# Linear attention, 32 heads: the last head's exp and relu of q cut into three parts, and new instruction orders on four engines

## The chip, the cores and the metric

The kernel runs on one core of a Trainium2 chip. The metric is the device time of one call in microseconds (us), lower is better. A run is called slow when it lies over 1.5% above the fastest run of the same kernel. "Ratio" is the mean time of one kernel's fast runs over that of the kernel before in the same rounds on the same chip, with a 95% interval; it is not quite the ratio of the medians that are quoted beside it. A profile is one execution; its span is 1.7 to 1.9 us shorter than the device time of the same execution.

## The reference, cut to what matters

```python
q, k, v: bf16, shape (1, 32, 2048, 128)          # 32 heads, 2048 rows, 128 columns
phi_q = where(q > 0, q + 1, exp(q)) + 1e-6       # the kernel: (min(exp(q), 1) + 1e-6) + max(q, 0)
phi_k = where(k > 0, k + 1, exp(k)) + 1e-6
kv  = einsum("bhsd,bhse->bhde", phi_k, v)        # one 128 x 128 matrix a head
z   = einsum("bhsd->bhd", phi_k)
num = einsum("bhqd,bhde->bhqe", phi_q, kv)
den = einsum("bhqd,bhd->bhq", phi_q, z) + 1e-6
return num / den
```

A head is 16 tiles of 128 rows. q, k, v and the output are 512 KB a head each, 67.1 MB in all.

## The kernel before

Every operation has a name such as `T12.0` (head 12, part 0). Each engine executes its own fixed list; semaphores carry the dependences between them. The names:

- SP (the queue of DMA): `ldq`, `ldk`, `ldv` load a head (seven buffers of each), `st` stores one (twelve buffers).
- TensorE (PE): `T` transposes q into PSUM, `kv` sums kv and z, `n` multiplies phi_q by them.
- ScalarE (ACT): `ek`, `eq` exp of k and q, `rqa` relu of the first half of q, `kvs` copies kv out of PSUM.
- VectorE (DVE): `em`, `emq` the min/add behind exp, `rkd`, `rqb` relu of half of k and of q, `r` reciprocal of the denominator, `f` the final multiply.
- GpSimd (POOL): `v1` copies v, `rkp` relu of the other half of k.

```python
NI, NO = 7, 12                                   # input and output buffers, in heads

def q_parts(h):
    return HALVES if h in (0, NH - 1) else WHOLE # HALVES = ((0, 8), (8, 16))

def gate(name, h):                               # GpSimd may start only when VectorE is here:
    if h < 3: return []
    return [f"r{h - 3}.0"] if name == "v1" else [f"f{h - 3}.0"]

# ... VectorE's list, heads 1 to 3 (the fill) and the end:
#   em1.0 r0.0 f0.0 rqb1 rkd2.0 emq1.0 rkd3.0 em2.0 r1.0 em3.0 rqb2 emq2.0 r0.1 f0.1
#   f1.0 rkd4.0 em4.0 rkd5.0 r1.1 rqb3 f1.1 ...
#   ... emq30.0 rqb31 r29.1 emq31.0 f29.1 r30.0 f30.0 r30.1 emq31.1 f30.1 r31.0 ... f31.2
# ... GpSimd's:  v12.0 v13.0 rkp3.0 v14.0 rkp4.0 ...
# ... SP's:      ... ldv12.0 ldq11.0 st1.0 st2.0 ldk13.0 ldv13.0 ldq12.0 ldk14.0 ...
#                ... ldv31.0 st18.0 st19.0 ldq31.0 st20.0 st21.0 ... st31.2

def load(name, dst, src, h, i, t0, t1, last):    # 'last': the buffer has been read
    add("SP", f"ld{name}{h}.{i}", lambda e: e.dma_start(dst[:, h % NI, t0:t1], ...), last, ...)

add("PE", f"T{h}.{i}", g, over("ldq", ...) + ["ident"]
    + ((every("eq", h - 1, q_parts) + rqs(h - 1)) if h else []))   # q loaded, PSUM read out
add("DVE", f"rqb{h}", ... rq_sb[:, h % NQ, n:], xT[:, n:], 0.0, None, op0=ALU.max ...)
```

## Time and profile before

The measurement gave 171.82 us (three runs, 171.63 to 172.05). The profiled run took 172.31 us, so it is one of the longer ones.

| stage of the profiled run | from, to (us) | what sets it |
|---|---|---|
| fill | 0 to 28.8 | loads of the first heads, then VectorE |
| steady | 28.8 to 156.4 | TensorE, 27 heads at 4.726 us |
| drain | 156.4 to 170.4 | VectorE's chain, then the last store |

These are lines of the page of the kernel before: the busy share of the DMA engines in tenths, in 40 slices of 4.26 us, and under it what they moved.

```profile
DMA  5999999999999999999999999999999999999874
GB/s 202 366 417 417 408 406 407 411 404 419 410 407 415 412 407 415 406 402 416 414 416 411 414 420 411 415 419 411 422 413 415 411 415 420 412 411 421 357 304 170
```

DMA is full from the third slice to the 37th, at about 412 GB/s, and falls in the last three.

The table of busy time by stage, of the same kernel, has a start and end in each row, then the length and the busy time of PE, PE's weight loads, DVE, ACT and POOL.

```profile
core 0: us, PE busy (x) PEld busy (x) DVE busy (x) ACT busy (x) POOL busy (x), PEclk, DMA share, GB/s
60.00:100.00 40.00, 40.00 (x732) 39.93 (x730) 39.51 (x70) 40.00 (x36) 22.63 (x17) 1.00 1.03 412
156.00:171.00 15.00, 8.09 (x145) 7.57 (x141) 11.07 (x21) 3.33 (x5) 0.20 (x1) 0.94 0.72 282
```

TensorE never pauses between 60 and 100 us.

The timeline has a start, a duration, then the engine and the instruction; in brackets stands the idle time ahead of it and what ended it. Line L352 holds the transposes, so its first instruction of a head is that head's start on TensorE. Shown are heads 2, 3, 4, 12 and 31, then the first numerator of head 31 and the last multiply.

```profile
16.81 1.07 PE L352 MATMUL la<-la 128*128 128x128 bf16 x16 [0.88 <-DVE la L364]
...
21.55 1.05 PE L352 MATMUL la<-la 128*128 128x128 bf16 x16
...
28.81 1.07 PE L352 MATMUL la<-la 128*128 128x128 bf16 x16 [1.22 <-DVE la L364]
...
66.62 1.05 PE L352 MATMUL la<-la 128*128 128x128 bf16 x16
...
156.40 0.61 PE L352 MATMUL la<-la 128*128 128x128 bf16 x8
...
163.38 0.18 PE L371 MATMUL la<-la 128*128 128x3 bf16 x1 [1.41 <-DVE la L392]
...
166.73 0.69 DVE L392 TENSOR_TENSOR la<-la 128x512 bf16<-128x512 f32 x1
```

Head 4 starts 7.26 us after head 3, against 4.73 in the steady state. The reason is on VectorE and GpSimd, in the same timeline (first the three VectorE instructions, then GpSimd's four of that time):

```profile
21.18 1.57 DVE L357 TENSOR_SCALAR la<-la 128x2048 bf16<-128x2048 bf16 x1
...
25.14 1.17 DVE L326 TENSOR_SCALAR la<-la 128x1024 bf16<-128x1024 bf16 x1
26.23 1.52 DVE L323 TENSOR_SCALAR la<-la 128x2048 bf16<-128x2048 bf16 x1
...
21.16 1.04 POOL L334 COPY la<-la 128x1024 int32<-128x1024 int32 x1 [2.58 <-DVE la L323]
22.17 1.47 POOL L330 TENSOR_SCALAR la<-la 128x1024 bf16<-128x1024 bf16 x1
24.99 1.04 POOL L334 COPY la<-la 128x1024 int32<-128x1024 int32 x1 [1.35 <-issue]
26.00 1.21 POOL L330 TENSOR_SCALAR la<-la 128x1024 bf16<-128x1024 bf16 x1
```

These are emq2, rkd4 and em4 (GpSimd's four are the copy of v3, rkp3, the copy of v4 and rkp4). Where nothing meets them, they take 0.62 to 0.69, 0.36 to 0.43 and 0.68 us; here each began while GpSimd was at work and ended after it. The Trainium skill ("SBUF — State Buffer", Who interferes with whom) says that VectorE in its two-port modes and GpSimd take a shared pair of ports as an exclusive lock for a whole instruction. The trace agrees: emq2 started at 21.18, GpSimd's copy ended at 22.20, and emq2 ended at 22.75, about its own 0.6 us later.

### The profile page before, as it was taken

Reading aid. Unit: us, or ns where it says so; the run is one execution under the profiler, and the core shown is the slowest. Engines: PE = TensorE matmul, PEld = TensorE weight load, DVE = VectorE, ACT = ScalarE, POOL = GpSimd, SP = SyncE. Lnnn points to the kernel's source line nnn. Section 1 sums busy time; section 2 is a strip of 40 time slices with the busy share of each in tenths; the row PEclk is TensorE's granted clock in tenths of the full one; section 3 lists DMA queues with packets and bytes.
Section 4 is the critical chain, followed back from the end, with each engine's and each line's share of the span. In section 5 each row is a group of like instructions: output and inputs, shape, how many; then the busy total and the mean of one; then the engine's idle time right before and its main releaser. Section 6 shows DMA issues by size and latency. Waiting matters only on the chain.

```text
span 170.4 us, 6325 instructions
## 1 busy us (share of the span) xinstructions
PE 159.1 (93%) x2775; PEld 153.7 (90%) x2775; DVE 155.3 (91%) x267; ACT 152.9 (90%) x132; POOL 86.1 (51%) x71
## 2 busy tenths in 40 slices
PE   6997977999999999999999999999999999999950
PEld 2677976999999999999999999999999999999940
DVE  0178999999999999999999999999999999999992
ACT  3699988899999999999999999999999999996700
POOL 1346364565456655556644566456665466654000
PEclk9999999999999999999999999999999999999998
DMA  5999999999999999999999999999999999999874
GB/s 202 366 417 417 408 406 407 411 404 419 410 407 415 412 407 415 406 402 416 414 416 411 414 420 411 415 419 411 422 413 415 411 415 420 412 411 421 357 304 170
DMA packets 18748, 67.53 MB, mean 396 GB/s; under 512 B 2080, under 2 KB 2464, under 8 KB 18720
## 3 DMA queue, kind: packets, MB, share of 16 engines
q1 hardware_dynamic: 18720, 67.12, 98.0%
q8 instruction: 22, 0.36, 0.8%
q14 instruction: 6, 0.05, 0.1%
HBM read 50.33 MB, written 16.78 MB: 394 GB/s over the span
## 4 chain that ended last, share of the span: by engine, by line
PE 83%; DVE 9%; ACT 4%; issue 1%; POOL 0%; POOLq 0%
PE la L341 30%; PE la L376 18%; PE la L352 16%; PE la L378 16%; DVE la L392 4%; ACT la L320 2%; PE la L299 2%; DVE la L323 1%; DVE la L364 1%; ACT la L355 1%; DVE la L357 1%; DVE la L326 1%; DVE la L385 1%; ACT la L361 1%; PE la L371 1%
## 5 line engine op out<-in xcount | busy, mean ns | idle before, releaser
L392 DVE TENSOR_TENSOR la<-la 128x1536 bf16<-128x1536 f32 (+2 forms) x65 | 77.7, 1196 | 0.4
L378 PE MATMUL la<-la 128*128 128x129 bf16 x512 | 68.1, 220 | 0.0
L376 PE MATMUL la<-la 128*128 128x129 bf16 x512 | 68.0, 219 | 0.0
L341 PE MATMUL la<-la 128*128 128x129 bf16 x1024 | 64.2, 219 | 0.0
L355 ACT ACTIVATE la<-la 128x2048 bf16<-128x2048 bf16 (+1 forms) x34 | 60.3, 1778 | 3.5 <-PE la L378 1.8
L334 POOL COPY la<-la 128x1024 int32<-128x1024 int32 (+1 forms) x33 | 40.9, 1242 | 42.2 <-DVE la L385 32.8
L320 ACT ACTIVATE la<-la 128x2048 bf16<-128x2048 bf16 (+1 forms) x33 | 61.3, 1862 | 0.0
L341 PEld LDWEIGHTS la<-la 128*128 128x128 bf16 x1024 | 60.0, 97 | 0.7 <-DVE la L290 0.5
L330 POOL TENSOR_SCALAR la<-la 128x1024 bf16<-128x1024 bf16 x32 | 44.6, 1395 | 27.1 <-DVE la L392 23.1
L378 PEld LDWEIGHTS la<-la 128*128 128x128 bf16 x512 | 49.5, 97 | 0.0
L376 PEld LDWEIGHTS la<-la 128*128 128x128 bf16 x512 | 47.1, 97 | 0.0
L352 PE MATMUL la<-la 128*128 128x128 bf16 x512 | 34.2, 220 | 2.1 <-DVE la L364 2.1
L361 ACT ACTIVATE la<-la 128x1024 bf16<-128x1024 bf16 x32 | 32.6, 1020 | 3.6 <-PE la L352 3.6
L371 PE MATMUL la<-la 128*128 128x3 bf16 (+1 forms) x192 | 32.3, 168 | 2.8 <-DVE la L392 2.4
L352 PEld LDWEIGHTS la<-la 128*128 128x128 bf16 x512 | 29.5, 98 | 3.2 <-DVE la L364 2.4
L323 DVE TENSOR_SCALAR la<-la 128x2048 bf16<-128x2048 bf16 (+1 forms) x33 | 23.4, 710 | 3.0 <-ACT la L320 3.0
L357 DVE TENSOR_SCALAR la<-la 128x2048 bf16<-128x2048 bf16 (+1 forms) x34 | 21.8, 644 | 0.0
L371 PEld LDWEIGHTS la<-la 128*128 128x128 bf16 x192 | 18.7, 97 | 3.4 <-DVE la L392 3.0
L364 DVE TENSOR_SCALAR la<-la 128x1024 bf16<-128x1024 bf16 x32 | 21.5, 673 | 0.2 <-ACT la L355 0.2
L326 DVE TENSOR_SCALAR la<-la 128x1024 bf16<-128x1024 bf16 x32 | 15.8, 492 | 5.7 <-DMA la<-in_k_dram 5.7
L385 DVE RECIPROCAL la<-la 128x12 f32<-128x12 f32 (+2 forms) x65 | 12.8, 198 | 2.6 <-PE la L378 1.0
L346 ACT ACTIVATE la<-la 128x129 bf16<-128x129 f32 x32 | 9.0, 282 | 0.3 <-PE la L341 0.3
(14 smaller groups left out, 11.7 us busy)
## 6 DMA issues: line engine op xcount, KB each, us to landing
la<-in_q_dram SPq DMA_DIRECT2D x32, 512.0 KB, 15.4
la<-in_k_dram SPq DMA_DIRECT2D x32, 512.0 KB, 15.5
la<-in_v_dram SPq DMA_DIRECT2D x32, 512.0 KB, 15.2
out_dram<-la SPq DMA_DIRECT2D x31, 512.0 KB, 15.2
out_dram<-la SPq DMA_DIRECT2D x2, 192.0 KB, 2.9
out_dram<-la SPq DMA_DIRECT2D x1, 128.0 KB, 2.2
```

The costliest lines, as they stand in the source:

```text
L320: add("ACT", f"ek{h}.{i}", lambda e, a=a, b=b: e.activation(em_sb[:, h % NE, a:b], k_sb[:, h % NI, a:b], ACT.Exp), over("ldk", h, ld_parts ...
L323: add("DVE", f"em{h}.{i}", lambda e, a=a, b=b: e.tensor_scalar(em_sb[:, h % NE, a:b], em_sb[:, h % NE, a:b], 1.0, EPS, op0=ALU.min, op1=AL ...
L330: add("POOL", f"rkp{h}.{i}", lambda e, a=a, b=b: e.tensor_scalar(rk_sb[:, h % NR, a:b], k_sb[:, h % NI, a:b], BIG, 0.0, op0=ALU.min, op1=A ...
L334: add("POOL", f"v1{h}.{i}", lambda e, a=a, b=b: e.tensor_copy(v1_sb[:, h % NV, a:b, 0:D].bitcast(i32), v_sb[:, h % NI, a:b].bitcast(i32)), ...
L341: ins = e.matmul(kv_ps, lhsT=src[:, j], rhs=v1_sb[:, h % NV, j, 0:NC], start=(j + part == 0), stop=(j == NT - 1 and part == 1))
L352: ins = e.transpose(xT[:, j], q_sb[:, h % NI, j], ident[:])
L355: add("ACT", f"eq{h}.{i}", lambda e, a=a, b=b: e.activation(emq_sb[:, h % NQ, a:b], xT[:, a:b], ACT.Exp), [f"T{h}.{i}"] + freed(NQ, h, ("n ...
L361: add("ACT", f"rqa{h}", lambda e: e.activation(rq_sb[:, h % NQ, 0:n], xT[:, 0:n], ACT.Relu), over("T", h, q_parts, 0, n) + freed(NQ, h, (" ...
L371: e.matmul(_ap(o_ps[:, :], o + D, [[NC, m]]), lhsT=ones[:], rhs=epsr[:, 0:m], start=True, stop=False, skip_group_check=True)
L376: e.matmul(to, lhsT=emq_sb[:, h % NQ, t], rhs=kvs_sb[:, h % NK], start=False, stop=False, skip_group_check=True)
L378: ins = e.matmul(to, lhsT=rq_sb[:, h % NQ, t], rhs=kvs_sb[:, h % NK], start=False, stop=True, skip_group_check=True)
L392: return e.tensor_tensor(out=_ap(o_sb[:, :, :, :], first(o_sb[:, h % NO, t0, 0:1]) - first(o_sb[:, :, :, :]), [[m * D, nb], [D, m], [1, D] ...
```

## The change

Its stated intent: for the last head, transpose in two halves, do exp in three parts beside the three tile groups, and split VectorE's share of the relu; and anneal all orders again "over more conditions". The diff, cut to its core:

```diff
 def q_parts(h):
-    return HALVES if h in (0, NH - 1) else WHOLE
+    return HALVES if h == 0 else ((0, 8), (8, 12), (12, 16)) if h == NH - 1 else WHOLE
+def t_parts(h):                                   # the transposes keep the two halves
+    return HALVES if h in (0, NH - 1) else WHOLE
+def rqb_parts(h): ...                             # last head: (8, 12), (12, 16); else as before

 "DVE":
-  ... r0.0 f0.0 rqb1 rkd2.0 emq1.0 rkd3.0 em2.0 r1.0 em3.0 rqb2 emq2.0 r0.1 f0.1 f1.0 rkd4.0 em4.0 rkd5.0 r1.1 rqb3 f1.1 ...
+  ... r0.0 rqb1.0 f0.0 rkd2.0 emq1.0 rkd3.0 em2.0 em3.0 rqb2.0 emq2.0 r0.1 f0.1 r1.0 rkd4.0 f1.0 em4.0 rqb3.0 r1.1 rkd5.0 f1.1 ...
-  ... emq30.0 rqb31 r29.1 emq31.0 f29.1 r30.0 f30.0 r30.1 emq31.1 f30.1 r31.0 ...
+  ... emq30.0 emq31.0 rqb31.1 r29.1 rqb31.0 f29.1 r30.0 f30.0 emq31.1 r30.1 emq31.2 f30.1 r31.0 ...
 "ACT":
-  rqa0 eq0.1 ek0.0 ek0.1 eq0.0 ek1.0 ...   eq31.1 eq31.0 kvs31 rqa31
+  eq0.0 eq0.1 ek0.0 ek0.1 rqa0 ek1.0 ...   eq31.0 eq31.1 eq31.2 kvs31 rqa31
 "POOL":
-  ... v12.0 v13.0 rkp3.0 v14.0 ...
+  ... v12.0 rkp3.0 v13.0 v14.0 ...
 "SP":   (re-ordered from the 14th load on; the two places that matter below; places count from 0)
-  ... ldq11.0 st1.0 st2.0 ldk13.0 ldv13.0 ldq12.0 ...                     (q of head 12: place 43)
+  ... ldv12.0 ldv13.0 ldv14.0 ldk13.0 ldk14.0 ldk15.0 ldv15.0 ldq12.0 ... (place 46)
-  ... ldv31.0 st18.0 st19.0 ldq31.0 st20.0 ...                            (q of head 31: place 115)
+  ... ldv31.0 st19.0 st20.0 ldq31.0 st21.0 ...                            (place 116)
```

TensorE's order stays, but for two equal warm-up pieces that change places.

More of the change, by code (lines that the diff above doesn't have):

```diff
@@ L65, in gate, with rqb_parts @@
     return [f"r{h - 3}.0"] if name == "v1" else [f"f{h - 3}.0"]
+BANK = ((0, 8), (8, 16))
+def t_parts(h):
+    return HALVES if h in (0, NH - 1) else WHOLE
+def rqb_parts(h):
+    if na(h) == 16:
+        return ()
+    if h == NH - 1:
+        return tuple(p for p in q_parts(h) if p[0] >= na(h))
+    return ((na(h), 16),)
 ORDER = {
     "PE": """
-        w2 w1 T0.0 T0.1 w0 kv0.0 kv0.1 T1.0 n0.0 kv1.0 kv1.1 T2.0 n0.1 n1.0 kv2.0 kv2.1 T3.0 n1.1 kv3.0 kv3.1 n2.0
+        w1 w2 T0.0 T0.1 w0 kv0.0 kv0.1 T1.0 n0.0 kv1.0 kv1.1 T2.0 n0.1 n1.0 kv2.0 kv2.1 T3.0 n1.1 kv3.0 kv3.1 n2.0
         T4.0 n2.1 kv4.0 kv4.1 n3.0 T5.0 n3.1 kv5.0 kv5.1 n4.0 T6.0 n4.1 kv6.0 kv6.1 n5.0 T7.0 n5.1 kv7.0 kv7.1 n6.0
@@ L81 @@
     "DVE": """
-        rkd0.0 v1ones0 v1ones1 eps0 ones em0.0 eps1 rkd1.0 em0.1 rqb0 eps2 emq0.0 emq0.1 em1.0 r0.0 f0.0 rqb1 rkd2.0
-        emq1.0 rkd3.0 em2.0 r1.0 em3.0 rqb2 emq2.0 r0.1 f0.1 f1.0 rkd4.0 em4.0 rkd5.0 r1.1 rqb3 f1.1 r2.0 emq3.0
-        f2.0 em5.0 r2.1 rqb4 f2.1 rkd6.0 r3.0 emq4.0 f3.0 em6.0 rqb5 r3.1 f3.1 emq5.0 r4.0 rkd7.0 f4.0 em7.0 r4.1
-        rqb6 f4.1 emq6.0 r5.0 rkd8.0 f5.0 em8.0 rqb7 r5.1 rkd9.0 f5.1 r6.0 emq7.0 f6.0 em9.0 r6.1 rqb8 f6.1 rkd10.0
-        r7.0 emq8.0 f7.0 em10.0 rqb9 r7.1 f7.1 rkd11.0 r8.0 emq9.0 f8.0 em11.0 r8.1 rqb10 f8.1 emq10.0 r9.0 rkd12.0
@@ L87 @@
-        f9.0 em12.0 r9.1 rqb11 f9.1 rkd13.0 r10.0 emq11.0 f10.0 em13.0 r10.1 rqb12 f10.1 emq12.0 r11.0 rkd14.0 f11.0
-        em14.0 rqb13 r11.1 rkd15.0 f11.1 r12.0 emq13.0 f12.0 em15.0 rqb14 r12.1 f12.1 rkd16.0 r13.0 emq14.0 f13.0
-        em16.0 r13.1 rqb15 f13.1 emq15.0 r14.0 rkd17.0 f14.0 em17.0 rqb16 r14.1 f14.1 emq16.0 r15.0 rkd18.0 f15.0
-        em18.0 rqb17 r15.1 rkd19.0 f15.1 r16.0 emq17.0 f16.0 em19.0 rqb18 r16.1 rkd20.0 f16.1 r17.0 emq18.0 f17.0
-        em20.0 rqb19 r17.1 rkd21.0 f17.1 r18.0 emq19.0 f18.0 em21.0 r18.1 rqb20 f18.1 emq20.0 r19.0 rkd22.0 f19.0
@@ L92 @@
-        em22.0 rqb21 r19.1 rkd23.0 f19.1 r20.0 emq21.0 f20.0 em23.0 r20.1 rqb22 rkd24.0 f20.1 r21.0 emq22.0 f21.0
-        em24.0 rqb23 r21.1 f21.1 rkd25.0 r22.0 emq23.0 f22.0 em25.0 rqb24 r22.1 rkd26.0 f22.1 r23.0 emq24.0 f23.0
-        em26.0 r23.1 rqb25 f23.1 emq25.0 r24.0 rkd27.0 f24.0 em27.0 r24.1 rqb26 f24.1 r25.0 emq26.0 f25.0 em28.0
-        rqb27 rkd28.0 r25.1 f25.1 r26.0 emq27.0 f26.0 em29.0 rqb28 r26.1 rkd29.0 f26.1 r27.0 emq28.0 f27.0 em30.0
-        rqb29 r27.1 rkd30.0 f27.1 r28.0 emq29.0 f28.0 em31.0 rqb30 r28.1 f28.1 r29.0 rkd31.0 f29.0 emq30.0 rqb31
@@ L97 @@
-        r29.1 emq31.0 f29.1 r30.0 f30.0 r30.1 emq31.1 f30.1 r31.0 f31.0 r31.1 f31.1 r31.2 f31.2
+        eps0 emq0.0 eps1 ones rkd0.0 v1ones0 em0.0 rkd1.0 em0.1 rqb0.0 eps2 emq0.1 v1ones1 em1.0 r0.0 rqb1.0 f0.0
+        rkd2.0 emq1.0 rkd3.0 em2.0 em3.0 rqb2.0 emq2.0 r0.1 f0.1 r1.0 rkd4.0 f1.0 em4.0 rqb3.0 r1.1 rkd5.0 f1.1 r2.0
+        emq3.0 f2.0 em5.0 rqb4.0 r2.1 rkd6.0 f2.1 r3.0 emq4.0 f3.0 em6.0 rqb5.0 r3.1 rkd7.0 f3.1 r4.0 emq5.0 f4.0
+        em7.0 rqb6.0 r4.1 rkd8.0 f4.1 r5.0 emq6.0 f5.0 em8.0 rqb7.0 r5.1 rkd9.0 f5.1 r6.0 emq7.0 f6.0 em9.0 rqb8.0
@@ new lines @@
+        r6.1 rkd10.0 f6.1 r7.0 emq8.0 f7.0 em10.0 rqb9.0 r7.1 rkd11.0 f7.1 r8.0 emq9.0 f8.0 em11.0 r8.1 rqb10.0 f8.1
+        rkd12.0 r9.0 emq10.0 f9.0 em12.0 rqb11.0 r9.1 rkd13.0 f9.1 r10.0 emq11.0 f10.0 em13.0 rqb12.0 r10.1 rkd14.0
+        f10.1 r11.0 emq12.0 f11.0 em14.0 r11.1 rqb13.0 f11.1 rkd15.0 r12.0 emq13.0 f12.0 em15.0 r12.1 rqb14.0 f12.1
+        rkd16.0 r13.0 emq14.0 f13.0 em16.0 rqb15.0 r13.1 rkd17.0 f13.1 r14.0 emq15.0 f14.0 em17.0 rqb16.0 r14.1
+        rkd18.0 f14.1 r15.0 emq16.0 f15.0 em18.0 r15.1 rqb17.0 f15.1 rkd19.0 r16.0 emq17.0 f16.0 em19.0 rqb18.0
@@ new lines @@
+        r16.1 rkd20.0 f16.1 r17.0 emq18.0 f17.0 em20.0 rqb19.0 r17.1 f17.1 emq19.0 r18.0 rkd21.0 f18.0 em21.0
+        rqb20.0 r18.1 rkd22.0 f18.1 r19.0 emq20.0 f19.0 em22.0 r19.1 rqb21.0 f19.1 emq21.0 r20.0 rkd23.0 f20.0
+        em23.0 rqb22.0 r20.1 rkd24.0 f20.1 r21.0 emq22.0 f21.0 em24.0 rqb23.0 r21.1 f21.1 r22.0 emq23.0 f22.0 em25.0
+        rqb24.0 r22.1 rkd25.0 f22.1 r23.0 emq24.0 f23.0 em26.0 rqb25.0 r23.1 rkd26.0 f23.1 r24.0 emq25.0 f24.0
+        em27.0 rqb26.0 r24.1 rkd27.0 f24.1 r25.0 emq26.0 f25.0 em28.0 rqb27.0 r25.1 f25.1 rkd28.0 r26.0 emq27.0
@@ L98 @@
+        f26.0 em29.0 rqb28.0 r26.1 rkd29.0 f26.1 r27.0 emq28.0 f27.0 em30.0 r27.1 rqb29.0 f27.1 rkd30.0 r28.0
+        emq29.0 f28.0 em31.0 r28.1 rqb30.0 f28.1 r29.0 rkd31.0 f29.0 emq30.0 emq31.0 rqb31.1 r29.1 rqb31.0 f29.1
+        r30.0 f30.0 emq31.1 r30.1 emq31.2 f30.1 r31.0 f31.0 r31.1 f31.1 r31.2 f31.2
     """,
     "ACT": """
-        rqa0 eq0.1 ek0.0 ek0.1 eq0.0 ek1.0 kvs0 eq1.0 rqa1 ek2.0 kvs1 ek3.0 eq2.0 rqa2 kvs2 ek4.0 eq3.0 kvs3 rqa3
+        eq0.0 eq0.1 ek0.0 ek0.1 rqa0 ek1.0 kvs0 eq1.0 rqa1 ek2.0 kvs1 ek3.0 eq2.0 rqa2 kvs2 ek4.0 eq3.0 kvs3 rqa3
@@ L106 @@
         ek26.0 eq25.0 kvs25 rqa25 ek27.0 eq26.0 kvs26 rqa26 ek28.0 eq27.0 kvs27 rqa27 ek29.0 eq28.0 kvs28 rqa28
-        ek30.0 eq29.0 kvs29 rqa29 ek31.0 eq30.0 kvs30 rqa30 eq31.1 eq31.0 kvs31 rqa31
+        ek30.0 eq29.0 kvs29 rqa29 ek31.0 eq30.0 kvs30 rqa30 eq31.0 eq31.1 eq31.2 kvs31 rqa31
     """,
     "POOL": """
-        ident0 ident rkp0.0 v10.0 v10.1 v11.0 rkp1.0 rkp2.0 v12.0 v13.0 rkp3.0 v14.0 rkp4.0 v15.0 rkp5.0 v16.0
+        ident0 ident rkp0.0 v10.0 v10.1 v11.0 rkp1.0 rkp2.0 v12.0 rkp3.0 v13.0 v14.0 rkp4.0 v15.0 rkp5.0 v16.0
         rkp6.0 v17.0 rkp7.0 v18.0 rkp8.0 v19.0 rkp9.0 v110.0 rkp10.0 v111.0 rkp11.0 v112.0 rkp12.0 v113.0 rkp13.0
@@ L116 @@
     "SP": """
-        ldq0.0 ldk0.0 ldv0.0 ldk1.0 ldq1.0 ldv1.0 ldk2.0 ldq2.0 ldk3.0 ldv2.0 ldk4.0 ldq3.0 ldv3.0 ldk5.0 ldq4.0
-        ldv4.0 ldk6.0 ldv5.0 ldq5.0 ldq6.0 ldv6.0 ldv7.0 ldq7.0 ldk7.0 ldk8.0 ldv8.0 ldk9.0 ldv9.0 st0.0 ldv10.0
-        ldq8.0 ldk10.0 ldq9.0 ldk11.0 ldk12.0 ldq10.0 ldv11.0 ldv12.0 ldq11.0 st1.0 st2.0 ldk13.0 ldv13.0 ldq12.0
-        ldk14.0 ldq13.0 ldv14.0 ldk15.0 ldq14.0 ldq15.0 ldv15.0 ldv16.0 ldq16.0 ldv17.0 ldq17.0 ldk16.0 ldk17.0
-        ldv18.0 ldk18.0 st3.0 ldq18.0 ldq19.0 ldk19.0 st4.0 ldk20.0 ldk21.0 ldq20.0 ldv19.0 ldk22.0 ldq21.0 ldq22.0
-        st5.0 ldv20.0 st6.0 ldv21.0 ldq23.0 ldk23.0 st7.0 ldq24.0 ldv22.0 ldk24.0 ldk25.0 ldv23.0 st8.0 st9.0
-        ldv24.0 ldv25.0 st10.0 ldq25.0 ldq26.0 ldk26.0 st11.0 st12.0 ldv26.0 ldk27.0 ldv27.0 ldk28.0 ldk29.0 ldq27.0
-        ldv28.0 ldv29.0 st13.0 ldk30.0 ldq28.0 st14.0 ldv30.0 ldq29.0 st15.0 ldk31.0 st16.0 st17.0 ldq30.0 ldv31.0
-        st18.0 st19.0 ldq31.0 st20.0 st21.0 st22.0 st23.0 st24.0 st25.0 st26.0 st27.0 st28.0 st29.0 st30.0 st31.0
+        ldq0.0 ldk0.0 ldv0.0 ldk1.0 ldq1.0 ldv1.0 ldk2.0 ldq2.0 ldk3.0 ldv2.0 ldk4.0 ldq3.0 ldv3.0 ldv4.0 ldq4.0
+        ldk5.0 ldv5.0 ldq5.0 ldq6.0 ldk6.0 ldv6.0 ldv7.0 ldv8.0 ldk7.0 ldk8.0 ldq7.0 ldv9.0 ldk9.0 ldq8.0 ldk10.0
+        ldq9.0 ldq10.0 st0.0 st1.0 ldv10.0 ldv11.0 ldq11.0 ldk11.0 ldk12.0 ldv12.0 ldv13.0 ldv14.0 ldk13.0 ldk14.0
+        ldk15.0 ldv15.0 ldq12.0 ldq13.0 ldv16.0 ldk16.0 ldv17.0 ldv18.0 ldq14.0 ldq15.0 st2.0 ldk17.0 ldv19.0
+        ldq16.0 ldq17.0 st3.0 ldq18.0 ldk18.0 ldq19.0 ldv20.0 ldk19.0 ldk20.0 ldk21.0 ldq20.0 st4.0 st5.0 st6.0
+        st7.0 ldq21.0 ldk22.0 ldv21.0 ldq22.0 st8.0 ldq23.0 ldk23.0 ldv22.0 ldv23.0 ldq24.0 ldq25.0 ldv24.0 ldk24.0
+        ldv25.0 st9.0 ldk25.0 st10.0 ldk26.0 ldv26.0 ldk27.0 st11.0 ldq26.0 st12.0 ldv27.0 st13.0 ldq27.0 ldv28.0
+        ldk28.0 ldq28.0 ldq29.0 ldk29.0 ldv29.0 ldk30.0 st14.0 ldq30.0 st15.0 ldv30.0 ldk31.0 st16.0 st17.0 st18.0
+        ldv31.0 st19.0 st20.0 ldq31.0 st21.0 st22.0 st23.0 st24.0 st25.0 st26.0 st27.0 st28.0 st29.0 st30.0 st31.0
         st31.1 st31.2
@@ L276, in fs, with rqs @@
                     if set(banks) & set(range(b0, b0 + nb))]
-        def rqs(h):
-            return ([f"rqa{h}"] if na(h) else []) + ([f"rqb{h}"] if na(h) < NT else [])
+        def rqs(h, t0=0, t1=NT):
+            return ([f"rqa{h}"] if t0 < na(h) else []) + over("rqb", h, rqb_parts, t0, t1)
         def rks(h, t0=0, t1=NT):
@@ L314, in head @@
             for i, (a, b) in enumerate(ld_parts(h)):
-                load("q", q_sb, qf, h, i, a, b, freed(NI, h, ("T", q_parts)))
+                load("q", q_sb, qf, h, i, a, b, freed(NI, h, ("T", t_parts)))
             for i, (a, b) in enumerate(ld_parts(h)):
@@ L347, in head @@
                 every("kv", h, kv_parts) + freed(NK, h, ("n", groups)))
-            for i, (a, b) in enumerate(q_parts(h)):
+            for i, (a, b) in enumerate(t_parts(h)):
                 def g(e, a=a, b=b):
@@ L354, in head @@
                 add("PE", f"T{h}.{i}", g, over("ldq", h, ld_parts, a, b) + ["ident"] + ((every("eq", h - 1, q_parts) + rqs(h - 1)) if h else []))
+            for i, (a, b) in enumerate(q_parts(h)):
                 add("ACT", f"eq{h}.{i}", lambda e, a=a, b=b: e.activation(emq_sb[:, h % NQ, a:b], xT[:, a:b], ACT.Exp),
-                    [f"T{h}.{i}"] + freed(NQ, h, ("n", groups)))
+                    over("T", h, t_parts, a, b) + freed(NQ, h, ("n", groups)))
                 add("DVE", f"emq{h}.{i}", lambda e, a=a, b=b: e.tensor_scalar(
@@ L361, in head @@
                 add("ACT", f"rqa{h}", lambda e: e.activation(rq_sb[:, h % NQ, 0:n], xT[:, 0:n], ACT.Relu),
-                    over("T", h, q_parts, 0, n) + freed(NQ, h, ("n", groups)))
-            if n < NT:
-                add("DVE", f"rqb{h}", lambda e: e.tensor_scalar(rq_sb[:, h % NQ, n:], xT[:, n:], 0.0, None, op0=ALU.max),
-                    over("eq", h, q_parts, n, NT) + freed(NQ, h, ("n", groups)))
+                    over("T", h, t_parts, 0, n) + freed(NQ, h, ("n", groups)))
+            for i, (a, b) in enumerate(rqb_parts(h)):
+                add("DVE", f"rqb{h}.{i}", lambda e, a=a, b=b: e.tensor_scalar(
+                    rq_sb[:, h % NQ, a:b], xT[:, a:b], 0.0, None, op0=ALU.max),
+                    over("eq", h, q_parts, *BANK[a // 8]) + freed(NQ, h, ("n", groups)))
             for i, (t0, nb, m, b0) in enumerate(groups(h)):
@@ L382, in head @@
                 t1 = t0 + nb * m
-                add("PE", f"n{h}.{i}", g, over("emq", h, q_parts, t0, t1) + [f"kvs{h}", "ones", "eps1", "eps2"] + rqs(h)
+                add("PE", f"n{h}.{i}", g, over("emq", h, q_parts, t0, t1) + [f"kvs{h}", "ones", "eps1", "eps2"] + rqs(h, t0, t1)
                     + (fs(h - 1, banks) if h else []) + ([f"kvs{h + 1}"] if 5 in banks and h + 1 < NH else []))
```

## The prediction

> **What bounds the kernel now.** Three stages. (1) Fill, 0 to 28.8 us: the timeline has TensorE's fifth transpose group (T4) starting at 28.81 us. Before it, TensorE waits in four places, 0.3 + 0.9 + 1.0 + 1.2 us, three of them for VectorE (relu line, output multiply). (2) Steady state, 28.8 to 156.4 us: 27 heads at 4.726 us each. TensorE is busy 40.00 of 40.00 us (table by stage, 60 to 100 us); a head is 1.84 us (kv) + 1.97 (numerator) + 0.91 (transposes), with no gap. VectorE (39.5) and ScalarE (40.0) are nearly as full, but ScalarE's head without waits took 4.63 us in the fill, so TensorE paces. (3) Drain, 156.4 to 170.4 us: VectorE runs almost without a gap from 154.6 to 167.4 us; then one store lands (about 2.2 us). DMA moves about 412 GB/s until 157 us, then slackens (357, 304, 170): some us to spare.
>
> **What the change does.** TensorE's order is unchanged in substance: stage 2 keeps 4.72 us a head.
>
> Last head: exp and its min/add in three parts, VectorE's relu in two. That adds one exp (ScalarE, idle then), one relu and one min/add on VectorE: from 0.39 us for eight tiles and 0.68 us for the eight-tile relu I estimate +0.1 to 0.2 us of VectorE work. The chain of the drain is n30.0 -> reciprocal -> multiply f30.0 (1.67 us) -> n31.0 (TensorE waits 1.41 us for f30.0) -> its reciprocals and multiplies. Splitting takes nothing off it. Drain: about 0, -0.2 to +0.2 us.
>
> Steady state: the rkd relu moves behind the multiply f.1, out of GpSimd's window. Before it lasts 0.53 to 0.57 us there, 0.36 us with GpSimd idle (156.8 us). The Trainium skill, "SBUF — State Buffer", Who interferes with whom, says a VectorE instruction in a two-port mode and GpSimd exclude each other for a whole instruction; the trace agrees (min/add that met a GpSimd instruction: 1.57 us instead of 0.62). It gives VectorE about 0.15 us a head, but not the time: TensorE paces.
>
> Fill: here is the gain. The relu of head 1 runs before f0.0 (T2 0.9 us earlier: 16.81 -> 15.9); rkp3 before v13 uses GpSimd's 2.58 us idle hole; the relu of head 3 comes before rkd5; v4's load is issued two places earlier. Walking the new orders by hand with the measured durations, T4 starts near 27.5 us instead of 28.81. One new collision (rkp3 with head 2's min/add) may take 0.7 us of T3 back.
>
> **Critical-path sum.** Fill -1.2 us (estimate), steady 0, drain 0, first 11 us 0: 171.82 - 1.2 = 170.6 us. Range 169.7 to 171.6. Faster by over 2% (below 168.4): 0.02; within 2%: 0.96; slower: 0.02.
>
> **What would show it.** Right: T4 starts 1 to 1.6 us earlier; 4.72 us a head between T4 and T31; VectorE's busy time falls by 3 to 5 us over the span, rkd's mean falling from 492 to about 400 ns; from n30.0's end to the span's end unchanged within 0.3 us. Wrong: T4 unmoved; TensorE waiting for DMA in the middle (loads reordered); or a drain shorter by over 0.5 us: then the last head's split was on the chain after all.
>
> **What could make it wrong.** ScalarE, within 2% of TensorE, may limit T5 and hand part of the gain back. DMA needs 444 GB/s at this pace but gives 412: the changed load order may run short near the end. Then the result is 171.5 to 172.

## The result and the profile after

The kernel after took 172.18 us (six runs, 171.90 to 172.41) against 171.78 us (six runs); the ratio is 1.0017 (0.9995 to 1.0038). Two later comparisons on other chips gave 0.9990 (0.9967 to 1.0013) and 0.9966 (0.9941 to 0.9991). So the change is worth nothing to a third of a per cent. The prediction was a gain of 1.2 us, with a range whose upper end was 171.6 us. The profiled run took 172.41 us, the longest of the six, as that of before was one of its longest; single profiles of one kernel differ, so most readings below are checked in further runs.

The timeline of the kernel after, for the same instructions (its transposes are on L368, numerators on L389, multiplies on L410):

```profile
15.76 1.06 PE L368 MATMUL la<-la 128*128 128x128 bf16 x16
...
21.68 1.06 PE L368 MATMUL la<-la 128*128 128x128 bf16 x16
...
27.01 1.05 PE L368 MATMUL la<-la 128*128 128x128 bf16 x16
...
65.62 1.05 PE L368 MATMUL la<-la 128*128 128x128 bf16 x16 [0.62 <-DMA la<-in_q_dram]
...
156.13 0.61 PE L368 MATMUL la<-la 128*128 128x128 bf16 x8 [0.59 <-DMA la<-in_q_dram]
...
163.11 0.18 PE L389 MATMUL la<-la 128*128 128x3 bf16 x1 [1.41 <-DVE la L410]
...
166.46 0.69 DVE L410 TENSOR_TENSOR la<-la 128x512 bf16<-128x512 f32 x1
```

The gain was there in the fill, and was handed back. Read down the column of starts and subtract the first list. Head 4 is 1.80 us earlier. Head 12 is only 1.00 us earlier, for it waited for its load of q: 65.62 is 5.47 us after head 11, not 4.73. Head 31 waited for its load likewise (5.46 us after head 30) and is 0.27 us earlier. From there to the last multiply both take the same 10.33 us, so that is 0.27 us earlier too, and the span is not shorter at all: 170.5 against 170.4 us.

The view of waits of the kernel after, from 30 us to the end, has the two waits together. Its columns are who waited for whom, us in total, times, and the longest.

```profile
PE la L368 <- DMA la<-in_q_dram: 1.2, 2, 0.6
```

The starts of the heads show 1.5 us of delay (0.74 us each), the idle time 1.2: it counts from the modelled end of the last matmul ahead of it, 0.22 us after its start, while matmuls are issued every 0.06 us.

VectorE and GpSimd in the fill of the kernel after, from the timeline (emq2, rkd4, em4; then copies and relus of GpSimd):

```profile
21.17 0.68 DVE L374 TENSOR_SCALAR la<-la 128x2048 bf16<-128x2048 bf16 x1
...
23.16 0.50 DVE L342 TENSOR_SCALAR la<-la 128x1024 bf16<-128x1024 bf16 x1
...
25.25 0.68 DVE L339 TENSOR_SCALAR la<-la 128x2048 bf16<-128x2048 bf16 x1
...
22.34 1.04 POOL L350 COPY la<-la 128x1024 int32<-128x1024 int32 x1 [1.20 <-DMA la<-in_v_dram]
23.70 1.04 POOL L350 COPY la<-la 128x1024 int32<-128x1024 int32 x1 [0.32 <-DVE la L342]
25.41 1.41 POOL L346 TENSOR_SCALAR la<-la 128x1024 bf16<-128x1024 bf16 x1 [0.67 <-DVE la L410]
```

The three collisions are all but gone: 1.86 us in the sum of the three instead of 4.26 (rkd4 still began beside a copy and took 0.50). The copy of v4 at 23.70 now runs beside a multiply (23.58 to 25.32 us), which reads PSUM. One new collision came, where the prediction feared one with head 2's min/add: here em3 was met, took 1.46 us (18.79 to 20.25) instead of 0.63, and head 3 starts 0.13 us later than in before.

DMA of the kernel after, as on the page:

```profile
DMA  5999999999999999999999999999999999999874
GB/s 213 336 421 414 407 405 411 406 410 405 409 420 408 409 406 404 414 414 419 410 407 415 413 423 412 406 416 412 419 414 416 417 413 420 413 413 417 359 314 172
```

It is the same as before. While the queue is full, a compute side that runs earlier meets the same landings (a second profile of after, below, shows it). This table (worked out from the issues and the landings in the traces, us) has both loads; the need is when the transposes would start at 4.725 us after those of the head before.

```
                          place   issued   landed   needed   landed before the need by
before  q of head 12       43      45.52    60.76    66.62        5.9
before  q of head 31      115     139.23   153.59   156.40        2.8
after   q of head 12       46      49.94    65.48    64.88       -0.6
after   q of head 31      116     141.18   156.00   155.40       -0.6
```

One place later cost q of head 31 2.4 us here, three places cost q of head 12 4.7 us. Over all profiles with whole stores q of head 31 landed at 153.6 to 154.3 us with it at place 115 (five) and at 155.3 to 156.0 with it at 116 (four), in the mean 1.8 us later. That is more than the 1.27 us that 512 KB take at 412 GB/s.

### The profile page after: what moved, and what is told of

Same layout as the page of the kernel before. It is cut to its first block, busy times and chain, and to the rows that moved or that the text cites. A ratio compares the mean times of both kernels' runs of the same rounds, so it can differ in the third digit from the quotient of the medians.

```text
span 170.5 us, 6328 instructions
## 1 busy us (share of the span) xinstructions
PE 159.4 (93%) x2775; PEld 153.7 (90%) x2775; DVE 153.3 (90%) x269; ACT 153.1 (90%) x133; POOL 87.0 (51%) x71
## 4 chain that ended last, share of the span: by engine, by line
PE 48%; DMA 22%; ACT 15%; issue 4%; DVE 4%; POOL 3%; SPq 2%; POOLq 0%
PE la L357 19%; DMA la<-in_q_dram 18%; PE la L394 10%; PE la L368 9%; PE la L396 9%; ACT la L336 6%; ACT la L372 5%; DMA la<-in_v_dram 4%; DVE la L410 3%; ACT la L378 3%; POOL la L350 2%; SPq L324 2%; POOL la L346 1%; ACT la L362 1%; DVE la L403 0%
## 5 line engine op out<-in xcount | busy, mean ns | idle before, releaser
L410 DVE TENSOR_TENSOR la<-la 128x1536 bf16<-128x1536 f32 (+2 forms) x65 | 77.7, 1195 | 0.3
L372 ACT ACTIVATE la<-la 128x2048 bf16<-128x2048 bf16 (+2 forms) x35 | 60.3, 1732 | 6.2 <-PE la L368 3.6
L350 POOL COPY la<-la 128x1024 int32<-128x1024 int32 (+1 forms) x33 | 41.7, 1267 | 40.4 <-DVE la L403 29.6
L336 ACT ACTIVATE la<-la 128x2048 bf16<-128x2048 bf16 (+1 forms) x33 | 61.4, 1863 | 0.0
L368 PE MATMUL la<-la 128*128 128x128 bf16 x512 | 34.1, 219 | 1.2 <-DMA la<-in_q_dram 1.2
L389 PE MATMUL la<-la 128*128 128x3 bf16 (+1 forms) x192 | 32.3, 168 | 2.4 <-DVE la L410 1.8
L368 PEld LDWEIGHTS la<-la 128*128 128x128 bf16 x512 | 29.6, 98 | 2.2 <-DVE la L342 0.8
L374 DVE TENSOR_SCALAR la<-la 128x2048 bf16<-128x2048 bf16 (+2 forms) x35 | 20.8, 596 | 5.8 <-ACT la L372 5.8
L339 DVE TENSOR_SCALAR la<-la 128x2048 bf16<-128x2048 bf16 (+1 forms) x33 | 23.3, 705 | 2.2 <-ACT la L336 2.2
L381 DVE TENSOR_SCALAR la<-la 128x1024 bf16<-128x1024 bf16 (+1 forms) x33 | 21.8, 661 | 1.9 <-ACT la L372 1.6
L389 PEld LDWEIGHTS la<-la 128*128 128x128 bf16 x192 | 18.7, 97 | 3.4 <-DVE la L410 2.4
L342 DVE TENSOR_SCALAR la<-la 128x1024 bf16<-128x1024 bf16 x32 | 15.0, 470 | 0.6 <-DMA la<-in_k_dram 0.6
```

The costliest lines, as they stand in the source:

```text
L336: add("ACT", f"ek{h}.{i}", lambda e, a=a, b=b: e.activation(em_sb[:, h % NE, a:b], k_sb[:, h % NI, a:b], ACT.Exp), over("ldk", h, ld_parts ...
L339: add("DVE", f"em{h}.{i}", lambda e, a=a, b=b: e.tensor_scalar(em_sb[:, h % NE, a:b], em_sb[:, h % NE, a:b], 1.0, EPS, op0=ALU.min, op1=AL ...
L350: add("POOL", f"v1{h}.{i}", lambda e, a=a, b=b: e.tensor_copy(v1_sb[:, h % NV, a:b, 0:D].bitcast(i32), v_sb[:, h % NI, a:b].bitcast(i32)), ...
L368: ins = e.transpose(xT[:, j], q_sb[:, h % NI, j], ident[:])
L372: add("ACT", f"eq{h}.{i}", lambda e, a=a, b=b: e.activation(emq_sb[:, h % NQ, a:b], xT[:, a:b], ACT.Exp), over("T", h, t_parts, a, b) + fr ...
L389: e.matmul(_ap(o_ps[:, :], o + D, [[NC, m]]), lhsT=ones[:], rhs=epsr[:, 0:m], start=True, stop=False, skip_group_check=True)
```

## The experiments

Theory A: the fill's gain is real, and DMA takes it back, first in two loads that the new order put late and then in the last stores. Rival B: bandwidth alone sets the end, whatever the order of loads. Rival C: another engine hands the gain back (VectorE, ScalarE). Open besides was which part of the change earns the fill's gain, and whether the last head's split is worth anything.

Each kernel was timed in six runs. The table has them all: start of head 4 and head 31 on TensorE, landing of q of head 31, start of the last multiply and what follows it in the profiled run, then the median and the ratio. At each rule another call begins, on another chip as far as was recorded, with the median of before in it. The median of a_light, 170.57, has the slow run in it; its five fast runs have 170.35.

```
kernel                  head 4  q31 lands  head 31  last mult.  rest   median  ratio (95% interval)
before                   28.81    153.59    156.40    166.73    3.67   171.78
after                    27.01    156.00    156.13    166.46    4.04   172.18  1.0017 (0.9995 to 1.0038)
--- before 171.72
a_two_loads              28.15    152.61    155.72    166.13    3.57   171.56  0.9985 (0.9956 to 1.0015)
a_sp_before              27.47    154.31    155.34    165.74    4.26   171.35  0.9975 (0.9941 to 1.0009)
b_sp_after               28.34    155.51    155.93    166.26    4.34   171.67  0.9987 (0.9962 to 1.0011)
b_split                  29.43    154.10    157.17    167.50    3.30   172.05  1.0006 (0.9982 to 1.0030)
--- before 171.99
after_again              27.74    155.99    156.12    166.46    4.04   171.86  0.9990 (0.9967 to 1.0013)
a_light                  27.60    146.04    155.18    165.58    3.32   170.57  0.9912 (0.9889 to 0.9935)
b_light                  27.04    145.63    154.80    165.13    3.67   171.91  0.9982 (0.9950 to 1.0014)
a_best                   27.30    153.33    155.09    165.49    5.01   172.10  1.0005 (0.9981 to 1.0028)
--- before 171.88
b_light_again            28.55    145.04    156.14    166.48    3.82   171.61  0.9973 (0.9937 to 1.0009)
b_gate_light             27.35    145.98    155.13    165.46    3.34   171.17  0.9956 (0.9918 to 0.9994)
b_relu1_light            27.57    144.96    155.28    165.61    3.29   171.09  0.9953 (0.9914 to 0.9992)
b_gate                   28.29    153.83    155.88    166.21    3.39   171.68  0.9988 (0.9965 to 1.0011)
--- before 172.16
a_nosplit_light          27.02    146.03    154.59    165.00    3.30   170.45  0.9911 (0.9888 to 0.9934)
a_oldpool_light          26.55    146.33    154.12    164.53    3.37   170.28  0.9888 (0.9862 to 0.9914)
a_oldsp_light            26.98    145.81    155.03    165.44    3.36   170.69  0.9916 (0.9897 to 0.9936)
b_newpool_sp_light       27.84    146.15    155.42    165.75    3.35   171.50  0.9960 (0.9938 to 0.9981)
--- before 172.19
b_dve                    27.55    153.85    155.46    165.86    3.84   171.46  0.9957 (0.9933 to 0.9981)
after_third              28.22    155.34    155.80    166.21    3.69   171.68  0.9966 (0.9941 to 0.9991)
```

### Two loads moved earlier

```diff
-  ... ldv12.0 ldv13.0 ldv14.0 ldk13.0 ldk14.0 ldk15.0 ldv15.0 ldq12.0 ldq13.0 ...
+  ... ldv12.0 ldq12.0 ldv13.0 ldv14.0 ldk13.0 ldk14.0 ldk15.0 ldv15.0 ldq13.0 ...
-  ... ldv31.0 st19.0 st20.0 ldq31.0 st21.0 ...
+  ... ldv31.0 ldq31.0 st19.0 st20.0 st21.0 ...
```

> The kernel after, with two loads moved earlier in the queue: q of head 12 from place 46 to 39, q of head 31 from 116 to 114. Theory A (two late loads ate the gain of the fill): transposes of head 12 start 4.72 us after those of head 11, transposes of head 31 near 154.7 us instead of 156.1, and the run takes 1.0 to 1.5 us less than after, about 170.8 us. Rival B (bandwidth: the last stores drain at the DMA's own rate, wherever TensorE stands): transposes of head 31 near 154.7 us too, but the end moves by less than 0.5 us, about 171.9 us. Rival C (VectorE or ScalarE hand the gain back): other waits take the place of the two, transposes of head 31 stay near 156.

The timeline of a_two_loads, heads 12 and 31:

```profile
65.95 1.05 PE L359 MATMUL la<-la 128*128 128x128 bf16 x16
...
155.72 0.61 PE L359 MATMUL la<-la 128*128 128x128 bf16 x8
```

Neither start has a wait for DMA any more, and head 31 starts 27 times 4.725 us after head 4. Rival C falls: no other wait took the place of the two. But head 31 came a us later than the expected 154.7, and the time fell short of A. One reason is in the profile: the fill of this run ended at 28.15 instead of 27.01 us, with the same orders, while the first loads landed at other times. The median, 171.56 us, lies nearer to B's 171.9 than to A's 170.8, and its ratio can't be told from those of after (0.9966 to 1.0017).

### The load order swapped between the two kernels

a_sp_before is after with the DMA queue of before; b_sp_after is before with the queue of after.

> The kernel after with the DMA queue in the order of before, all else as after. Theory A: no wait of TensorE for a load in the middle, transposes of head 31 near 154.7 to 155.0 us, 170.8 us. Rival B (drain at the DMA's rate): same place of head 31, end at 171.6 or more. Rival C: head 31 near 156.

> The kernel before with the DMA queue in the order of after. Theory A: TensorE is 1.8 us later there, so q of head 12 (landing at about 65.5 us, needed at 66.6) and q of head 31 (156.0, needed at 156.4) are just in time: no wait, same time as before within 0.3 us, 171.8 us. If the load order were bad in itself: two waits of about 0.7 us each, 173.0 us or more.

With the old queue head 31 had no wait for a load, as A expected, and was 1.06 us earlier than in before (155.34), a third of a us later than expected. The time, 171.35 us, is between A's 170.8 and B's 171.6. The last multiply was 0.99 us earlier than in before. Yet the span was only 0.4 us shorter (170.0), because 4.26 us followed the last multiply instead of 3.67. The late order costs the kernel before nothing: 171.67 us, no wait of TensorE for a load after 30 us. In it, q of head 31 landed at 155.51 and was needed at 155.93. A queue order is late only for a compute side fast enough to notice.

### The last head's split alone

b_split is before with the three parts of exp and min/add and the two of relu, and the short order that they need at the end; all else stays.

> The kernel before with the last head's split alone (exp and min/add in three parts, relu of VectorE in two), all other orders as before. Prediction on record: nothing, -0.2 to +0.2 us, since the chain from the numerator of head 30 to the end has no split part on it. If the split is worth what the change's name says: 0.5 us or more off, and a shorter way from the transposes of head 31 to the last multiply (11.0 us in before).

The timeline of b_split, head 31 and the last multiply:

```profile
157.17 0.61 PE L367 MATMUL la<-la 128*128 128x128 bf16 x8
...
167.50 0.69 DVE L409 TENSOR_TENSOR la<-la 128x512 bf16<-128x512 f32 x1
```

They are 10.33 us apart, as in before (156.40, 166.73) and in after (156.13, 166.46). The ratio is 1.0006. The part that gave the change its name moves nothing, as predicted: the chain runs from head 30's numerators through f30.0 (1.7 us on VectorE) to head 31's, past the parts that were split.

### Less work for DMA

The two kernels with only one of sixteen rows of tiles stored for heads 0 to 7. The result is wrong (those rows stay unwritten); semaphores, orders and engine instructions are the same.

```diff
-  e.dma_start(rows(of, h)[:, a:b], o_sb[:, h % NO, a:b])
+  e.dma_start(rows(of, h)[:, a:b if h >= 8 else a + 1], o_sb[:, h % NO, a:b if h >= 8 else a + 1])
```

> The kernel after, but the stores of heads 0 to 7 write one row of tiles out of sixteen (wrong result on purpose; DMA has some 3.9 MB, about 9.5 us, less to move; every semaphore, order and engine instruction stays). If DMA (late loads and the last stores) ate the gain: no wait of TensorE for a load, transposes of head 31 27 x 4.725 us after those of head 4, and this kernel 1.0 to 1.6 us faster than the kernel before with the same light stores; about 169.5 to 170.3 us. If the engines ate it: no more than 0.4 us faster than that one.

> The kernel before with the same light stores of heads 0 to 7 (wrong result on purpose). If the last stores of before were at the DMA's limit too: up to 0.5 us faster than before. If TensorE and the drain's chain alone set it: as before, 171.2 to 171.8 us.

This separates the theories. With 3.9 MB of 67.1 less to move, after takes 170.35 us (five fast runs) and before 171.91: the change is worth 1.6 us at the medians, and 1.2 in the ratios (0.9912 against 0.9982). The difference is as expected; both times are up to 0.1 us above the expected ranges. With whole stores the same change was worth -0.4 to 0.5 us. Before gains next to nothing from light stores (0.9982, 0.9973 when repeated); after gains 1.5 us on the same chip (171.86 to 170.35). So DMA hardly limits before, and does limit after. Here q of head 31 landed 9 us ahead of its need, and 3.3 us followed the last multiply of after instead of 4.0.

The profiled run of b_light, 170.59 us, was that kernel's best; its six runs range from 170.6 to 172.3. A single profile would have told the opposite: head 4 at 27.04, earlier than in a_light. In that run v3 and v4 landed about a us later than in before's profile (22.0 and 26.0 against 21.1 and 24.9 us), so GpSimd's copies missed VectorE's instructions. In this profile the later loads went with the shorter fill. a_light's fast runs are 170.2 to 170.8 us; its slow one took 172.9.

### After once more, and the last stores in pieces

> The kernel after once more, on the same chip as the others of this call: a second profile of the fill and a comparison. Theory A: q of head 31 lands at 155.5 to 156.1 us again, whatever the fill did (a third of a us later than TensorE was ready, or more); fill 0.8 to 1.8 us shorter than before; 171.8 to 172.2 us.

q of head 31 landed at 155.99 us in this second profile and at 156.00 in the first; head 31 started at 156.12 and 156.13, though the fill ended 0.7 us apart (27.74 and 27.01). So the landing pins the start. (The view of waits puts this wait down to VectorE, 0.5 us, whose reciprocal it shows as last; by the kernel the transposes don't wait for a reciprocal, but for this load.)

a_best is a_two_loads with the stores of heads 28 to 30 cut in two, each piece issued when its multiply is done:

> The kernel after with q of head 12 and of head 31 earlier in the queue and the stores of heads 28 to 30 in two pieces (12 and 4 tiles), each issued when its multiply is done. If the last stores queue up behind each other on the slowest DMA engine: the last landing comes 0.4 to 0.8 us sooner after the last multiply than with whole stores (2.1 us there), and the run takes 170.6 to 171.1 us. If not: 171.4 us as with the two loads alone.

This failed, and is worth a look. The last multiply came 1.24 us earlier than in before, the earliest of the kernels that store everything, and the last landing did not come earlier: 5.01 us followed instead of 3.67. The expected saving at the end did not come. A likely reason is in the landing events of single transfers. The Trainium skill ("DMA: Bandwidth & Descriptors", Why a DMA increments its semaphore by 16 and not by 1) says that up to 16 engines work on one transfer and finish independently. The traces agree, and show how far apart they drift (us, the first and the last of the sixteen):

```
                          before             after
q of head 2          12.7 to  14.4      13.0 to  14.4
q of head 12         58.5 to  60.8      62.5 to  65.5
q of head 31        148.7 to 153.6     150.2 to 156.0
store of head 28    160.0 to 164.8     160.2 to 166.0
store of head 29    163.7 to 166.2     163.4 to 167.2
store of head 30    166.8 to 168.4     166.6 to 168.5
store of head 31.2  169.2 to 169.7     168.8 to 169.8
```

Around 155 us the slowest engine is 5 to 6 us behind the fastest. A transfer counts as landed with the slowest. In after its landings are 1.2 to 1.3 us apart from head 28's store to the end, the pace of a full queue (512 KB at 412 GB/s is 1.27 us). This fits a slowest engine that is full to the end, while the sum over the 16 falls from 157 us on. In before there are gaps of 1.4 and 2.2 us among those landings, as if its slowest engine had to wait for stores. The landings don't name their engine, so that it is one and the same engine all along is inferred.

The other profiles bear on rival B. Of the eleven with whole stores, nine show the steady 1.2 to 1.3 us from head 27's store to head 30's; before and b_split, whose last multiplies come latest (166.73 and 167.50 us), alone have a gap of over 2 us. With light stores the last landing follows the end of the last multiply by 1.9 us in seven of nine profiles. In the nine with whole stores it follows by 1.9 (b_gate) to 3.6 us (a_best), 2.6 in both after and after_again. So B is right in part: in most of these runs the end waits for landings, and an earlier multiply doesn't bring it forward by as much. The two late loads do hold TensorE back, but to remove them alone bought no time clear of noise.

### Which part of the fill's orders earns the gain

Before with light stores once more, as the base, and three kernels with a small edit of before, with light stores or whole ones:

```diff
 b_gate, b_gate_light:
-  em2.0 r1.0 em3.0 rqb2 emq2.0 r0.1 f0.1 f1.0 rkd4.0 em4.0
+  em2.0 em3.0 rqb2 emq2.0 r0.1 f0.1 r1.0 rkd4.0 f1.0 em4.0
 b_relu1_light:
-  r0.0 f0.0 rqb1 rkd2.0
+  r0.0 rqb1 f0.0 rkd2.0
```

> The kernel before with light stores again, as the base of the next two, for a second profile and on the same chip. Theory A: 171.3 to 172.2 us, widely spread from run to run (by about 1.5 us), as the fill's collisions of VectorE and GpSimd come and go with the landing of the loads of v3 and v4.

> Before with light stores, and in VectorE's order two things moved: the reciprocal r1.0, which opens GpSimd's gate for the copy of v4, behind the multiply f0.1, and the relu rkd4 in front of f1.0. If the fill's gain is that GpSimd's copy then runs beside f1.0 (which reads PSUM) and no longer meets rkd4 and the min/add em4: those two take 0.4 and 0.7 us instead of 1.2 and 1.5, transposes of head 4 start 5.3 to 5.8 us after those of head 3, 170.6 to 171.2 us, and less spread. If the gain comes from the relu of head 1 or of head 3: no change against before with light stores.

> Before with light stores, and the relu of head 1 in front of f0.0. The prediction on record counted it as a part of the gain. Transposes of head 2 near 15.9 instead of 16.9 us. In all profiles with it head 3 was not earlier, so I expect head 3 at 21.6 to 22.8 us and no change of the time within 0.4 us; if it was a part of the gain, 0.5 us or more faster than before with light stores.

> Before with the moved reciprocal and relu alone, whole stores, right result. If the last stores' drain is the floor at about 171.2 to 171.5 us: in that range, however early the fill ends; last multiply ends 0.5 to 1.3 us sooner than in before and the last landing follows it by 2.3 us or more. If there is no such floor: 170.8 us or less.

These are inconclusive. The base repeated with 171.61 us, spread from 170.3 to 172.5. In b_gate_light's profile rkd4 and em4 took 0.71 (0.4 was expected) and 0.68 us and head 4 came 5.54 us after head 3, as expected, but its runs still range from 170.3 to 172.2. In b_relu1_light head 2 started at 15.77 us, as expected, head 3 at 21.65, within the range of the others; 171.09 us is between "nothing" and "a part", with runs from 170.2 to 172.3. b_gate missed the expected range from above: 171.68 us, and its profile shows new collisions (the min/add of head 1 took 1.53, the relu rkd5 1.25 us). One edit moves collisions about; it doesn't remove them.

So the change was taken apart in larger pieces, with light stores:

> After with light stores, without the last head's split. If the split is worth nothing (11.02 us from head 31's transposes to the last multiply's start plus its 0.69 us with and without it): 170.3 to 170.8 us, as with it. If the split earns the gain: 171.2 us or more.

> After with light stores and GpSimd's order of before (copy of v3 ahead of the relu of head 3). If GpSimd's order is a part of the gain: 171.0 us or more and a spread like before's (170.3 to 172.3). If VectorE's order suffices: 170.2 to 170.9 us.

> After with light stores and the load order of before (v4 lands about 25 instead of 22.5 us). With light stores no load is late in either order: 170.2 to 170.9 us, unless v4's earlier landing is what keeps the copy of v4 away from VectorE's SBUF operations; then 171.0 or more.

> Before with light stores and with GpSimd's order and the load order of after, VectorE's order of before. If VectorE's order earns the gain: as before with light stores, 171.3 to 172.0 us, widely spread. If the other two orders do: 170.3 to 170.9 us.

Three kernels keep VectorE's order of after and lose one other part each: the split, GpSimd's order, the load order. They take 170.45, 170.28 and 170.69 us (0.9911, 0.9888, 0.9916), with spreads of 0.7 to 1.3 us. The one that gets GpSimd's order and the load order but keeps VectorE's old order takes 171.50 us (0.9960). VectorE's order (with the first five instructions of ScalarE's that go with it) earns the gain; no other part is needed for it. GpSimd's new order shows no gain (170.28 us without it, 170.35 with it in a_light, on different chips).

### VectorE's order alone, with whole stores

> The kernel before with VectorE's order of after (and ScalarE's first five instructions), nothing else: load order, GpSimd's order, last head as before; right result. VectorE's order earns the fill's 1.3 us: transposes of head 4 at 26.5 to 27.6 us, no wait of TensorE for a load, transposes of head 31 at 154.1 to 155.2 us. The last stores on the slowest DMA engine then decide: 171.0 to 171.5 us, 0.2 to 0.6 us under before, not the 1.3 of the light stores. Without such a floor: 170.5 us.

> The kernel after on the same chip: q of head 31 lands at 155.5 to 156.1 us and head 31's transposes wait for it; 171.7 to 172.2 us, 0.3 to 0.8 us over the kernel with VectorE's order alone.

b_dve is before with VectorE's order of after and ScalarE's first five instructions, nothing else. It gives the right result in 171.46 us, ratio 0.9957 (0.9933 to 0.9981): faster than before by 0.4%, which is clear of noise but small. The timeline of b_dve, heads 4 and 31:

```profile
27.55 1.07 PE L335 MATMUL la<-la 128*128 128x128 bf16 x16
...
155.46 0.61 PE L335 MATMUL la<-la 128*128 128x128 bf16 x8
```

No wait for a load is between them; the 0.3 us over 27 times 4.725 is a wait for VectorE just after head 4. Head 31 came 0.3 us later than expected. With light stores VectorE's order brings 0.8 to 1.2 us (from 171.50 to between 170.28 and 170.69), here 0.7 at the medians; the time is at the upper end of the expected range and a little further under before than expected. In the profile 3.84 us followed the last multiply instead of the 3.3 of the light kernels with this order, so the last stores took about half a us of the gain. Against after on the same chip (171.68 us, 0.9966) it is 0.2 us ahead, less than the expected 0.3 to 0.8 and too little to tell them apart. In that third profile of after, the fill happened to end late (28.22 us), q of head 31 landed at 155.34, and there was no wait for it, against the expectation.

## Why the prediction was wrong

It foresaw 170.6 us, and 172.18 came. Point by point:

- "Fill -1.2 us": right in size. Head 4 started 1.8 us earlier in the first pair of profiles. Over all profiles, it started at 26.6 to 28.2 us (mean 27.4 of eleven) with VectorE's order of after and at 27.0 to 29.4 (mean 28.3 of six) with that of before; the timed gain with DMA out of the way was 1.2 to 1.6 us (a_light against b_light).
- "Walking the new orders": right sum, partly wrong parts. It credited GpSimd's rkp3 and the earlier load of v4; taken out, neither cost time. It credited the relu of head 1, which brings head 2 forward by about a us; head 3 then starts no earlier. What remained is VectorE's order as a whole. That it earns its gain by avoiding GpSimd is not shown: in b_dve's fill rkd4 still took 1.21 and em4 1.08 us, though head 4 came 1.26 us earlier than in before. The relu of head 3 ahead of rkd5, which the prediction also credited, was never tried alone.
- "Steady 0": the pace held at 4.72 us a head, but with two waits for loads of q, which took 1.5 us of the fill's 1.8 (0.8 in the second profile of after, none in the third, whose fill ended later; head 31 started at 156.13, 156.12 and 155.80). **This is the step that failed.** The prediction said of DMA that it has "some us to spare", read from the falling GB/s of the last slices, and gave the new load order no cost in the sum. It named the danger at its end (loads short "near the end", 171.5 to 172 us) and gave it too little weight. The margin could have been read from the trace before: q of head 31 landed 2.8 us ahead of its need, the predicted gain takes 1.2 of that, and one place later takes 1.3 more by an estimate from 512 KB at 412 GB/s. That left 0.3 us, too thin to be counted as nothing; as it ran, the place cost 2.4 us. With less for DMA to move the gain came out in the time (1.2 to 1.6 us), which shows that DMA, not another engine, took it.
- "Drain 0": right for compute. From head 31's transposes to the last multiply it is 10.33 us in both, and in b_split. Wrong for what follows: the span ended 3.67 us after the start of the last multiply in before, 4.04 in after, and 5.01 where compute was earliest. With light stores it was 3.3 to 3.8. The same failed step, "some us to spare", lies behind this: the last landings are a second limit, not foreseen. How the loss divides between the two late loads and the last stores was not measured.
- "VectorE's busy time falls by 3 to 5 us, rkd's mean from 492 to about 400 ns": the direction was right, the size too large: it fell by 2.0 us (155.3 to 153.3), and the mean to 470 ns, a quarter of the way.

These are the groups of rkd on the two pages, in the columns count, busy us, mean ns of one, and the idle time before. Before:

```profile
L326 DVE TENSOR_SCALAR la<-la 128x1024 bf16<-128x1024 bf16 x32 | 15.8, 492 | 5.7 <-DMA la<-in_k_dram 5.7
```

After:

```profile
L342 DVE TENSOR_SCALAR la<-la 128x1024 bf16<-128x1024 bf16 x32 | 15.0, 470 | 0.6 <-DMA la<-in_k_dram 0.6
```

The Trainium skill ("Perfetto Trace Analysis", What "DMA-bound" means) says that a kernel can be bound by specific DMA engines. The landings fit that, and the sum over the engines can hide it: on the pages of before and after alike it falls (357, 304, 170 and 359, 314, 172 GB/s), while the last pieces of after's stores landed every 1.2 to 1.3 us.

What stays open: why the first loads land so differently from run to run (v of head 2 at 15.8 to 18.7 us) and so shuffle the fill; which DMA engine falls behind, whether it is always the same one, and why the last landings are late by such different amounts (1.9 to 3.6 us after the last multiply); and which of the moves in VectorE's order matter most, and by what. The runs also do not settle how much of the 0.8 to 1.2 us between b_dve (171.46) and the light kernels with VectorE's order is late stores and how much the chip and chance.

## What to carry to other kernels

When a saturated DMA queue feeds a saturated engine, ask of each load how long before its need it lands; a gain ahead of it is worth at most that margin, and a load moved back by one place costs one transfer of it or more (here 1.8 us in the mean for one place, with 1.27 for a transfer). Don't read a falling sum of DMA bandwidth as slack without a further look: look at when the last of the sixteen pieces of each transfer lands. And to see whether an engine's gain is hidden or absent, take bytes away from both kernels and time them again, in many runs: one profile of a fill that depends on landing times can show either answer.

## What the Trainium skill lacked or had wrong

- "DMA: Bandwidth & Descriptors": it says that the engines of a transfer finish independently, not how far they drift. Here the first and last of sixteen pieces were 1.8 us apart at 14 us and 4.9 us apart at 153 us (before), 5.8 us at 156 us (after).
- The same page, Where 436 GB/s comes from, says that for transfers between HBM and SBUF the HBM side (about 358 GB/s) binds. Read by itself this is wrong for a program on one core, which moved 402 to 423 GB/s in all full slices here; the page's own 425 GB/s for a large transfer, which it marks as a single-core number, fits better.
- "SBUF — State Buffer" says that who starts first has the ports for an instruction. It doesn't say who is next. In before, emq2 waited for the first of two back-to-back GpSimd instructions (ended 22.20 us) and ended at 22.75, while the second, started at 22.17, took 1.47 instead of the 1.04 us of its shortest: this fits VectorE going ahead of it.
- No page of those read says that a single collision's place depends on when a load lands. Head 4 started anywhere from 27.0 to 29.4 us with VectorE's order of before.
